# Block means by a dense load and VectorE instead of crossbar turns, in a sparse-attention and GEGLU kernel

## The chip, the cores and the metric

One core of a Trainium2 chip. The metric is the device time of one execution in microseconds (us), as the median of several runs. Lower is better. PE is TensorE's matmul side, PEld its weight loads, DVE is VectorE, ACT is ScalarE, POOL is GpSimd and SP is SyncE, which only issues DMAs here.

## What is computed

Attention over 4 batches, 8 heads, 768 positions and 64 dimensions, then a gated feed-forward layer over the 3072 tokens:

```
k_sum = k.reshape(B, H, nb, 32, D).max(axis=3)
v_sum = v.reshape(B, H, nb, 32, D).mean(axis=3)
scores_l = where(|i - j| < 16, scale * q k^T, -1e9)
scores_s = scale * q k_sum^T + log(32)
a = softmax(concat(scores_l, scores_s))
x = a @ concat(v, v_sum)                     # heads joined: 3072 x 512
out = x + sigmoid(x @ w_res) * ((gelu(x @ w_gate) * (x @ w_val)) @ w_out)
```

The change concerns `v_sum`: the mean of v over each block of 32 positions, 24 blocks for each head.

## The kernel before

Work goes by units of 384 tokens, two to a batch (`NU` = 8, unit u is half u % 2 of batch u // 2). The order of the instructions on every engine is written out by hand in the loop over u (line 532), and each engine works through its own in that order. In iteration u the feed-forward layer of unit u runs, and the attention of unit n = u + 1 is laid between its matmuls.

The iteration starts with twelve fo steps (`fo_step`, L407): for each slice of 128 of the 1536 hidden columns, four matmuls with w_gate (g) and four with w_val (vv) by TensorE, a Gelu by ScalarE (L404), and the product gvT by VectorE (L405). PSUM has four banks ("mm") for g, vv, r, f and part of the scores, taken in turn; so the banks of an fo step are wanted again two steps later. After each fo step `values_step` (L451) and some lines of the loop add work for the next batch. After the twelve steps come, for the next unit, scores (`s_step`: matmuls into s, exponential by ScalarE into P, `mask_part` on VectorE, L347), the product with the values (`av_step`: ao by TensorE, reciprocal and multiplication by VectorE, giving xn), and for the current unit r (L416), f (L432) and the end (`end_step`, L435: two VectorE instructions and the store of 128 rows of out). x must stand transposed (xT) for the next unit's matmuls: either TensorE turns it and ScalarE copies it (`xt_step`, L378), or the DMA crossbar does (`xt_dma`, L385, issued by SP). The first is used for all of x of units 0 to 3, the second for three of four head pairs from unit 4 on (`if u < 3 ... else`, L657); from u = 4 on the first matmuls of a unit (L548) also take the head pair that comes last at the end.

The values and their block means live in `vext[b % 2]`, a tile of 128 rows for each group of 64 queries: 96 rows hold the 96 values in reach, rows 96 to 127 the block means of the batch, the same in each of the 12 groups. `load_values` (L96) loads the values, `v_spread` (L287) copies those which two groups share, and `vsum_bc` (L296) copies the means to the groups, half of the groups at a time. Rows of P over the 24 real blocks are held at zero by a bias of -30000, so what stands in rows 120 to 127 has no weight.

For batches 0 and 1 the means come from TensorE (`vsum_sum`). For batches 2 and 3 they come by this path: `load_rows` (L171) loads v as rows of positions into `v_sb`, eight DMAs of 256-byte pieces issued by POOL; `turn_values` (L258) turns it by four crossbar DMAs into vT in the first fo step of u = 2 or 4; `block_sums` (L265) sums over blocks in fo steps 8 to 11 of the same unit, one head pair at a time; `turn_sums` (L270) turns the sums back by one more crossbar DMA in the first fo step of u = 3 or 5, and `vsum_bc` scales and copies them to the rows of vext: to the first six groups in fo steps 5 to 8 of u = 3 or 5, and to the other six in fo steps 2 to 5 of u = 4 or 6.

k and q are loaded as rows by the same `load_rows` and turned by the crossbar (`turn_batch`, L246: two DMAs for k and one for q for each of the four head pairs). `k_rest` (L206) is five VectorE instructions on a head pair of k: the maxima of the blocks and the copies at the edges of the groups. For batches 2 and 3 three head pairs are turned in u = 2 or 4 and the fourth in u = 3 or 5, and k_rest runs in fo steps 0, 2, 4 and 11 of u = 3 or 5.

POOL issues all loads, in order; a load starts behind a small copy (`gate`, L168) that holds POOL until a given gvT is there. Batch 2 is loaded from u = 1, fo 6 on; batch 3's rows from the end of the fo steps of u = 2 on, and its values at the start of u = 3. POOL also issues the stores of out for u = 3 to 6, SP those of the other units.

Of the kernel before, what the change touches and what calls it, by code (L numbers as in the profile page):

```python
# [9 lines left out]
BF16 = mybir.dt.bfloat16  # L10
# [5 lines left out]
def kernel(  # L16
# [11 lines left out]
    nc = tc.nc  # L28
    B, H, S, D = q.shape
# [45 lines left out]
    vext = [const.tile([128, NT, H, D + 1], BF16, name=f"vext{i}") for i in range(2)]  # L75
    vsum = [const.tile([128, H, D + 1], BF16, name=f"vsum{i}") for i in range(2)]
    tick = const.tile([1, 1], BF16, name="tick")
    vsT = const.tile([128, NP, 128], BF16, name="vsT")
    vsB = const.tile([128, NP, 128], BF16, name="vsB")
    w_gate = wpool.tile([128, KO, DFF], BF16, name="w_gate")  # L80
    w_val = wpool.tile([128, KO, DFF], BF16, name="w_val")
    w_out = wpool.tile([128, FO, DM], BF16, name="w_out")
# [16 lines left out]
        dst = vext[b % 2][0 if c else WIN:128, 2 * c, :, 0:D] if c < NC else vext[b % 2][64:64 + WIN, NT - 1, :, 0:D]  # L99
        nc.gpsimd.dma_start(out=dst, in_=v[b, :, lo:hi, :].rearrange("h p d -> p h d"))  # L100

    k_sb, q_sb, v_sb, vT = {}, {}, {}, {}

    with tc.manual_schedule():

# [63 lines left out]
            nc.gpsimd.tensor_copy(tick[:], t)  # L169

        def load_rows(b):  # L171
            for sb, src, name in ((k_sb, k, "k_sb"), (q_sb, q, "q_sb"), (v_sb, v, "v_sb"))[0:2 if b == 1 else 3]:
                sb[b] = (qk1 if sb is v_sb else qk).tile([128, NP, NC, 2 * D], BF16, tag=name, name=name)
                for h in range(H) if b > 1 else (4, 5, 6, 7, 0, 1, 2, 3):
                    nc.gpsimd.dma_start(out=sb[b][:, h // 2, :, h % 2 * D:h % 2 * D + D],  # L175
                                        in_=src[b, h].rearrange("(c p) d -> p c d", c=NC))

        def load_batch(b):
            load_rows(b)
# [75 lines left out]
                    out=qT[b % 2][hp].rearrange("d (c m) -> d c m", c=NC),  # L255
                    in_=q_sb[b][:, hp].rearrange("p c d -> p (c d)"))

        def turn_values(b):  # L258
            vT = qk1.tile([128, NP, S], BF16, tag="k0", name="vT")
            for hp in range(NP):  # L260
                nc.sync.dma_start_transpose(out=vT[:, hp].rearrange("d (c m) -> d c m", c=NC),
                                            in_=v_sb[b][:, hp].rearrange("p c d -> p (c d)"))
            return vT

        def block_sums(vT, hp):  # L265
            with nc.allow_low_precision("block means are bf16 operands"):
                nc.vector.tensor_reduce(out=vsT[:, hp, 96:96 + NB], in_=vT[:, hp].rearrange("d (n w) -> d n w", w=BLK),
                                        axis=mybir.AxisListType.X, op=ALU.add)

        def turn_sums():  # L270
            nc.sync.dma_start_transpose(out=vsB[:], in_=vsT.rearrange("d p n -> d (p n)"))

        def vsum_sum(b, pool, tag, chunks=range(NC + 1), vs=None, first=True, last=False):
            if vs is None:
# [20 lines left out]

        def vsum_bc(b, hp, lo, hi):  # L296
            dst = vext[b % 2][96:128, lo:hi, 2 * hp:2 * hp + 2, 0:D]
            if b < 2:
                src = vsum[b][96:128, 2 * hp:2 * hp + 2, 0:D]
                nc.vector.tensor_copy(dst, src.unsqueeze(1).to_broadcast([32, hi - lo, 2, D]))  # L300
            else:
                src = vsB[96:128, hp].rearrange("p (h d) -> p h d", d=D)
                nc.vector.tensor_scalar_mul(dst, src.unsqueeze(1).to_broadcast([32, hi - lo, 2, D]), 1.0 / BLK)

        def s_tiles(two=None):
            if two:
# [128 lines left out]
        def end_step(u, st, sub, c0=0, c1=DM):  # L435
            f, th = st["f", sub], st["th", sub][:, c0:c1]
            nc.vector.scalar_tensor_tensor(th, th, 1.0, f[:, 0:c1 - c0], ALU.add, ALU.mult)  # L437
            o = work.tile([128, DM], F32, tag="o", name="o")
            nc.vector.scalar_tensor_tensor(o[:, 0:c1 - c0].rearrange("p (k d) -> p k d", d=128),  # L439
                                           th.rearrange("p (k d) -> p k d", d=128), 0.5,  # L440
                                           st["xn"][:, c0 // 128:c1 // 128, sub, :], ALU.mult, ALU.add)
            row = u * TU + sub * 128
            (nc.gpsimd if 2 < u < NU - 1 else nc.sync).dma_start(out=out[row:row + 128, c0:c1], in_=o[:, 0:c1 - c0])  # L443

        def keep_warm(n, wp=None):
            if wp is None:
# [4 lines left out]
        def values_step(u, fo):  # L451

            b = u // 2 + 1
            if u in (2, 4) and fo >= FO - NP:
                block_sums(vT[b], fo - FO + NP)
            if u in (3, 5):
                if fo in (1, 3):
                    v_spread(b, 0, HT // 2, fo // 2)
                if 5 <= fo < 9:
                    vsum_bc(b, fo - 5, 0, HT)  # L460
            if u % 2 == 0 and u < NU - 1:
                if fo in (0, 1):
                    v_spread(b - 1, HT // 2, NC, fo)
                if 2 <= fo < 2 + NP:
                    vsum_bc(b - 1, fo - 2, HT, NT)


# [64 lines left out]
        for u in range(NU):  # L532
# [2 lines left out]
            n = u + 1  # L535
            if u == 1:
                turn_batch(1, 2, NP)
            if u == 3:
                for c in range(NC + 1):
                    load_values(3, c)  # L540
            gvT = upool.tile([128, FO, TU], BF16, tag="gvT", name="gvT")
            if u > 3:
                firsts = [(w, fo, ps_mm.tile([128, 512], F32, tag="mm", name="gv"))
                          for w, fo in ((w_gate, 0), (w_val, 0), (w_gate, 1))]
                for kos in ((0, 1, 3), (2,)):
                    for w, fo, acc in firsts:
                        for ko in kos:
                            nc.tensor.matmul(acc[:, 0:TU], w[:, ko, fo * 128:(fo + 1) * 128], st["xT"][:, ko, :],  # L548
                                             start=(ko == 0), stop=(ko == 2), skip_group_check=True)
            for fo in range(FO):  # L550
                if u == 0 and fo < 2:
                    for w, _, acc in firsts[2 * fo:2 * fo + 2]:
                        half_fo(st, w, fo, KO - 1, KO, acc)
                    fo_end(gvT, fo, firsts[2 * fo][2], firsts[2 * fo + 1][2])
                elif u > 3 and fo == 0:
                    fo_end(gvT, fo, firsts[0][2], firsts[1][2])
                elif u > 3 and fo == 1:
                    fo_end(gvT, fo, firsts[2][2], half_fo(st, w_val, fo, 0, KO))
                else:
                    fo_step(st, gvT, fo)  # L560
                values_step(u, fo)
                if u == 0 and fo == 4:
                    nc.vector.memset(vsT[:], 0.0)
                    load_rows(1)
                if u == 0 and fo == 6:
                    vext_consts(1)
                if u == 0 and fo == FO - 1:
                    kw_consts(1)
                    for c in range(NC + 1):
                        load_values(1, c)  # L570
                if u == 2 and fo == FO - 1:
                    gate(gvT[0:1, fo, 0:1])
                    load_rows(3)
                if half == 0 and 1 < nb < B and fo == 0:
                    vT[nb] = turn_values(nb)
                    turn_batch(nb, 0, NP - 1)
                if half == 1 and 1 < nb < B and fo == 0:
                    turn_sums()
                    turn_batch(nb, NP - 1, NP)
                if half == 1 and 1 < nb < B and fo in (0, 2, 4, 11):  # L580
                    k_rest(kW[nb % 2][(0, 2, 4, 11).index(fo)])
                if u == 1 and fo == 6:
                    gate(gvT[0:1, fo, 0:1])
                    load_batch(2)
                if u == 1 and fo in (1, 2, 6, 7):
                    home = TT if fo % 2 else AO
                    if fo < 4:
                        k_step(nb, fo - 1, *home)
                    else:
                        q_step(q_sb[nb], nb, 0, S, fo - 6, *home)  # L590
                if u == 1 and fo == FO - 1:
                    k_rest(kW[1][2])
                    k_rest(kW[1][3])
                if u == 0 and fo >= FO - 4:
                    k_later(kW[0][fo - FO + 4])
                if u == 0 and fo in (FO - 3, FO - 2):
                    for hp in range(2 * (fo - FO + 3), 2 * (fo - FO + 3) + 2):
                        q_step(qb, 0, TU, S, hp, *(TT if hp % 2 else AO))
# [55 lines left out]
            av_step(n, 1, nst, *TT)  # L654
            s_step(n, 2, nst)
            s_step(n, 3, nst, two=(MM, MM), masked=False)
            if u < 3:  # L657
                if u > 1:
                    end_step(u, st, 0)
                mask_part(3, nst)  # L660
                m = 6 if u > 1 else 9
                ffn_step(st, gvT, 1, 0 if u > 1 else 6, m)
                xt_step(n, 0, nst, *AO, nc.scalar.copy)
                ffn_step(st, gvT, 1, m, FO)
                xt_step(n, 1, nst, *TT, nc.scalar.copy)
                res_step(st, 2)
                av_step(n, 2, nst, *AO)
# [5 lines left out]
            else:  # L673
# [2 lines left out]
                mask_part(3, nst)  # L676
                end_step(u, st, 0)
                ffn_step(st, gvT, 1, 0, FO)
                av_step(n, 2, nst, *AO)
                xt_dma(2, nst)  # L680
                av_step(n, 3, nst, *TT)
# [37 lines left out]
```

The softmax here doesn't subtract the row's maximum and nothing guards it: scores larger than these inputs give would overflow.

## Time and profile before

| | |
|---|---|
| median of 3 runs | 260.31 us (258.98, 260.31, 260.67) |
| the profiled execution | 259.77 us, of which the span from the first to the last instruction is 257.9 us |
| granted TensorE clock | 1.0 of full speed |
| busy, share of the span | PE 97%, DVE 69%, PEld 54%, ACT 50%, POOL 39% |
| DMA bytes | 30.16 MB in 117899 packets, of which 104816 under 512 bytes |
| chain that ended last, by engine | PE 79%, DVE 7%, DMA 5%, POOL 4%, issue 2%, ACT 1% |

The span begins with the first instruction and ends with the last. Units begin, by the first matmul of their fo steps, at about 24.1 (u = 0), 51.7, 84.2, 113.1, 142.4, 170.7, 199.4 and 227.7 us (u = 7). In the lines of a timeline the first two numbers are the start and the duration in us, then the engine, the source line, the operation, what is written and what is read, and the count; in brackets the idle time before it and what ended it. A group's line names the operation and ends with busy us, mean ns of one instruction, and the idle time before it. Durations of instructions that follow each other can overlap, since VectorE and TensorE are pipelined: the pace is the distance from start to start. In the chain of waits overlaps are taken out.

### The profile page before, as it was taken

What the parts mean: (1) busy time and instruction counts of PE and PEld (TensorE: products, weight loads), DVE (VectorE), ACT (ScalarE), POOL (GpSimd) and SP (SyncE); (2) the same over time, 40 slices, a digit from 0 to 9 for tenths busy, and PEclk for the clock granted to TensorE, in tenths of its full rate; (3) what the DMA queues carried; (4) which work ended last, traced back from release to release, by engine and by line L of the source; (5) the groups of instructions that cost most, each with busy time, mean ns of one, the idle gap of its engine ahead of it and who ended that gap; (6) DMA issues with size and microseconds to landing.
All of it is one profiled execution on the core that took longest, in us unless ns stands there. A gap on an engine that the chain in (4) does not pass through costs nothing.

```text
span 257.9 us, 5755 instructions
## 1 busy us (share of the span) xinstructions
PE 250.2 (97%) x2249; PEld 139.5 (54%) x2249; DVE 178.3 (69%) x426; ACT 129.5 (50%) x223; POOL 101.0 (39%) x139
## 2 busy tenths in 40 slices
PE   7989999999999999999999999999999999999993
PEld 3546555566545555555554565555554665556543
DVE  5756866595598878679959768679768853764333
ACT  4855369455635637553373537453473537443310
POOL 7995542795699910996650100020001000010000
PEclk9999999999999999999999999999999999999999
DMA  7999999999999999999994995165003200130012
GB/s 157 151 151 193 199 202 199 142 209 123 151 152 165 179 129 167 125 186 202 154 134 90 146 145 103 31 153 68 1 3 86 84 0 0 33 137 3 1 41 83
DMA packets 117899, 30.16 MB, mean 117 GB/s; under 512 B 104816, under 2 KB 115504, under 8 KB 117872
## 3 DMA queue, kind: packets, MB, share of 16 engines
q0 software_dynamic: 86640, 19.11, 86.7%
q1 hardware_dynamic: 31232, 10.69, 25.6%
q8 instruction: 17, 0.28, 0.5%
q14 instruction: 10, 0.08, 0.1%
HBM read 32.51 MB, written 6.29 MB: 150 GB/s over the span
## 4 chain that ended last, share of the span: by engine, by line
PE 79%; DVE 7%; DMA 5%; POOL 4%; issue 2%; ACT 1%; POOLq 0%; DVEq 0%
PE f L432 22%; PE vv L398 19%; PE g L398 18%; PE r L416 8%; PE ao L362 3%; DMA k_sb<-in_k_dram 3%; PE gv L548 3%; DMA vext<-in_v_dram 2%; PE s L330 2%; DVE gvT L405 2%; PE xp L381 1%; POOL k_sb L175 1%; POOL vext L100 1%; DVE ks L211 1%; DVE vext L294 1%
## 5 line engine op out<-in xcount | busy, mean ns | idle before, releaser
L398 PE MATMUL vv<-xT,w_val 128*128 128x384 bf16 x364 | 74.5, 326 | 0.1
L404 ACT ACTIVATE ge<-g 128x384 f32<-128x384 f32 x87 | 42.7, 491 | 63.3 <-PE g L398 37.0
L398 PE MATMUL g<-xT,w_gate 128*128 128x384 bf16 x348 | 71.3, 326 | 0.4 <-DVE gvT L405 0.2
L405 DVE TENSOR_TENSOR gvT<-ge,vv 128x384 bf16<-128x384 f32 x91 | 50.0, 553 | 27.5 <-PE vv L398 25.5
L432 PE MATMUL f<-w_out,gvT 128*128 128x512 bf16 (+2 forms) x312 | 68.4, 363 | 0.0
L398 PEld LDWEIGHTS <-w_val 128*128 128x128 bf16 x368 | 36.0, 98 | 24.0 <-issue 0.4
L398 PEld LDWEIGHTS <-w_gate 128*128 128x128 bf16 x352 | 34.1, 98 | 23.2 <-issue 1.1
L432 PEld LDWEIGHTS <-gvT 128*128 128x128 bf16 x312 | 28.3, 98 | 28.2
L443 POOL DMA_DIRECT2D out_dram<-o x12 | 6.5, 544 | 90.9 <-DVE rz L370 76.0
L422 ACT ACTIVATE th<-r 128x512 f32<-128x512 f32 x24 | 14.2, 602 | 24.8 <-PE r L416 24.8
L437 DVE SCALAR_TENSOR_TENSOR th<-th,f 128x512 f32<-128x512 f32 (+2 forms) x26 | 16.7, 642 | 12.3 <-PE f L432 8.5
L175 POOL DMA_DIRECT2D k_sb<-in_k_dram x24 | 19.8, 839 | 12.5 <-DMA w_out<-in_moe_w_out_dram 5.2
L416 PE MATMUL r<-w_res,xT 128*128 128x512 bf16 x96 | 24.4, 380 | 0.0
L100 POOL DMA_DIRECT2D vext<-in_v_dram x28 | 23.2, 875 | 1.5 <-PE g L398 1.2
L175 POOL DMA_DIRECT2D q_sb<-in_q_dram x24 | 20.0, 875 | 1.6 <-DMA k_sb<-in_k_dram 1.4
L347 DVE TENSOR_TENSOR P<-P,maskt 128x768 bf16<-128x768 bf16 x28 | 15.3, 556 | 7.2 <-ACT P L336 3.9
L372 DVE TENSOR_TENSOR xn<-ao,rz 128x384 bf16<-128x384 f32 x32 | 17.8, 558 | 1.1
L383 ACT COPY xT<-xp 128x384 bf16<-128x384 bf16 x20 | 9.3, 482 | 16.5 <-PE xp L381 14.8
L439 DVE SCALAR_TENSOR_TENSOR o<-th,xn 128x512 f32<-128x512 f32 (+2 forms) x26 | 16.9, 651 | 0.9
L336 ACT ACTIVATE P<-s,bias_t 128x384 bf16<-128x384 f32 x32 | 16.8, 579 | 1.3 <-PE s L330 1.3
L339 ACT ACTIVATE P<-s,bias_t 128x768 bf16<-128x768 f32 x16 | 14.5, 904 | 3.5 <-PE s L330 3.4
L175 POOL DMA_DIRECT2D v_sb<-in_v_dram x16 | 13.2, 850 | 2.8 <-DMA q_sb<-in_q_dram 2.5
(99 smaller groups left out, 236.0 us busy)
## 6 DMA issues: line engine op xcount, KB each, us to landing
out_dram<-o POOLq DMA_DIRECT2D x12, 256.0 KB, 2.4
out_dram<-o SPq DMA_DIRECT2D x11, 256.0 KB, 4.2
vext<-in_v_dram POOLq DMA_DIRECT2D x20, 128.0 KB, 7.4
k_sb<-in_k_dram POOLq DMA_DIRECT2D x24, 96.0 KB, 7.7
q_sb<-in_q_dram POOLq DMA_DIRECT2D x24, 96.0 KB, 5.5
w_gate<-in_moe_w_gate_dram POOLq DMA_DIRECT2D x6, 256.0 KB, 8.5
w_val<-in_moe_w_val_dram POOLq DMA_DIRECT2D x6, 256.0 KB, 9.1
w_out<-in_moe_w_out_dram POOLq DMA_DIRECT2D x3, 512.0 KB, 14.9
```

Source lines behind the costliest of these rows:

```text
L100: nc.gpsimd.dma_start(out=dst, in_=v[b, :, lo:hi, :].rearrange("h p d -> p h d"))
L175: nc.gpsimd.dma_start(out=sb[b][:, h // 2, :, h % 2 * D:h % 2 * D + D], in_=src[b, h].rearrange("(c p) d -> p c d", c=NC))
L336: nc.scalar.activation(P[:, hh].rearrange("p t q -> p (t q)"), s[hh][:, 0:TU], AF.Exp, scale=scale, bias=bias_t[:])
L347: nc.vector.tensor_mul(Pf, Pf, maskt.unsqueeze(1).to_broadcast([128, 2 * HT, QT]))
L372: nc.vector.tensor_mul(xn, ao[:, :, :, 0:D], rz.to_broadcast([128, NSUB, 2, D]))
L398: nc.tensor.matmul(acc[:, 0:TU], w[:, ko, fs], st["xT"][:, ko, :], start=(ko == 0), stop=(ko == KO - 1))
L404: nc.scalar.activation(ge[:], g[:, 0:TU], AF.Gelu)
L405: nc.vector.tensor_mul(gvT[:, fo, :], ge[:], vv[:, 0:TU])
L416: nc.tensor.matmul(r[:], st["xT"][:, ko, ss], w_res[:, ko, :], start=(ko == 0), stop=(ko == KO - 1))
L432: nc.tensor.matmul(st["f", sub][:, 0:c1 - c0], gvT[:, fo, ss], w_out[:, fo, c0:c1], start=(fo == 0), stop=(fo == FO - 1))
L437: nc.vector.scalar_tensor_tensor(th, th, 1.0, f[:, 0:c1 - c0], ALU.add, ALU.mult)
L439: nc.vector.scalar_tensor_tensor(o[:, 0:c1 - c0].rearrange("p (k d) -> p k d", d=128), th.rearrange("p (k d) -> p k d", d=128), 0.5, st["x ...
```

## The change

- The row load of v, its crossbar turns, and the turn of the sums are gone. `v_sb` for batches 2 and 3 has one partition for each pair of head and block (4 heads x 24 blocks = 96) and for each of two groups of heads, with the 32 x 64 values of the block one after the other: two DMAs from POOL, whose rows are dense in memory.
- `block_means` sums over the 32 positions on VectorE, a quarter of the work in each of fo steps 8 to 11 of u = 2 and 4, and a second instruction scales the means and writes them six times, for six groups of queries.
- `spread_means` puts them on their rows of vext by eight plain DMAs from SP, one for each head: for the first six groups in fo step 2 of u = 3 and 5, for the other six in fo step 0 of u = 4 and 6. `vsum_bc` is left for batches 0 and 1 only.
- `v_spread` in u = 3 and 5 moves from fo steps 1 and 3 to 2 and 7.
- All four head pairs of k and q are turned in the first fo step of u = 2 and 4. `k_rest` of pair 0 moves to the end of u = 2 and 4, in front of the last two av_step; that of the others is in fo steps 0, 4 and 11 of u = 3 and 5.
- Batch 3 is loaded, all together, from u = 3, fo 0 on.
- x of unit 3 goes by `xt_dma` for three of four head pairs, in the order that later units have; the first matmuls of u = 3 are ordered as those of later units are.
- The stores of out of u = 2 go by POOL.

```diff
-    vsT = const.tile([128, NP, 128], BF16, name="vsT")
-    vsB = const.tile([128, NP, 128], BF16, name="vsB")
+    vds = const.tile([PP, 2, D], BF16, name="vds")
+    vdt = const.tile([128, 2, HT, D], BF16, name="vdt")
...
-            for sb, src, name in ((k_sb, k, "k_sb"), (q_sb, q, "q_sb"), (v_sb, v, "v_sb"))[0:2 if b == 1 else 3]:
-                sb[b] = (qk1 if sb is v_sb else qk).tile([128, NP, NC, 2 * D], BF16, tag=name, name=name)
+            for sb, src, name in ((k_sb, k, "k_sb"), (q_sb, q, "q_sb")):
+                sb[b] = qk.tile([128, NP, NC, 2 * D], BF16, tag=name, name=name)
...
+            if b > 1:
+                v_sb[b] = qk1.tile([PP, 2, BLK, D], BF16, tag="k0", name="v_sb")
+                for g in range(2):
+                    nc.gpsimd.dma_start(out=v_sb[b][:, g].rearrange("p w d -> p (w d)"),
+                                        in_=v[b, 4 * g:4 * g + 4].rearrange("h (n w) d -> (h n) (w d)", w=BLK))
...
-        def block_sums(vT, hp):
+        def block_means(b, i):
+
+            g, d = i // 2, slice(i % 2 * 32, i % 2 * 32 + 32)
             with nc.allow_low_precision("block means are bf16 operands"):
-                nc.vector.tensor_reduce(out=vsT[:, hp, 96:96 + NB], in_=vT[:, hp].rearrange("d (n w) -> d n w", w=BLK),
+                nc.vector.tensor_reduce(out=vds[0:PP, g, d], in_=v_sb[b][:, g, :, d].rearrange("p w d -> p d w"),
                                         axis=mybir.AxisListType.X, op=ALU.add)
-        def turn_sums():
-            nc.sync.dma_start_transpose(out=vsB[:], in_=vsT.rearrange("d p n -> d (p n)"))
+            nc.vector.tensor_scalar_mul(vdt[0:PP, g, :, d], vds[:, g, d].unsqueeze(1).to_broadcast([PP, HT, 32]), 1.0 / BLK)
+
+        def spread_means(b, lo, hi):
+
+            for h in range(H):
+                nc.sync.dma_start(out=vext[b % 2][96:128, lo:hi, h, 0:D],
+                                  in_=vdt[h % 4 * NB:h % 4 * NB + 32, h // 4])
...
-            (nc.gpsimd if 2 < u < NU - 1 else nc.sync).dma_start(out=out[row:row + 128, c0:c1], in_=o[:, 0:c1 - c0])
+            (nc.gpsimd if 1 < u < NU - 1 else nc.sync).dma_start(out=out[row:row + 128, c0:c1], in_=o[:, 0:c1 - c0])
...
             if u in (2, 4) and fo >= FO - NP:
-                block_sums(vT[b], fo - FO + NP)
-            if u in (3, 5):
-                if fo in (1, 3):
-                    v_spread(b, 0, HT // 2, fo // 2)
-                if 5 <= fo < 9:
-                    vsum_bc(b, fo - 5, 0, HT)
+                block_means(b, fo - FO + NP)
+            if u in (3, 5) and fo in (2, 7):
+                v_spread(b, 0, HT // 2, fo // 7)
+                if fo == 2:
+                    spread_means(b, 0, HT)
             if u % 2 == 0 and u < NU - 1:
                 if fo in (0, 1):
                     v_spread(b - 1, HT // 2, NC, fo)
-                if 2 <= fo < 2 + NP:
+                    if fo == 0 and u > 2:
+                        spread_means(b - 1, HT, NT)
+                if 2 <= fo < 2 + NP and u < 4:
                     vsum_bc(b - 1, fo - 2, HT, NT)
...
-            if u == 3:
-                for c in range(NC + 1):
-                    load_values(3, c)
...
-            if u > 3:
+            if u > 2:
                 firsts = [(w, fo, ps_mm.tile([128, 512], F32, tag="mm", name="gv"))
...
-                if u == 2 and fo == FO - 1:
+                if u == 3 and fo == 0:
                     gate(gvT[0:1, fo, 0:1])
-                    load_rows(3)
+                    load_batch(3)
                 if half == 0 and 1 < nb < B and fo == 0:
-                    vT[nb] = turn_values(nb)
-                    turn_batch(nb, 0, NP - 1)
-                if half == 1 and 1 < nb < B and fo == 0:
-                    turn_sums()
-                    turn_batch(nb, NP - 1, NP)
-                if half == 1 and 1 < nb < B and fo in (0, 2, 4, 11):
-                    k_rest(kW[nb % 2][(0, 2, 4, 11).index(fo)])
+                    turn_batch(nb, 0, NP)
+                if half == 1 and 1 < nb < B and fo in (0, 4, 11):
+                    k_rest(kW[nb % 2][(0, 4, 11).index(fo) + 1])
...
-            if u < 3:
-                if u > 1:
-                    end_step(u, st, 0)
+            if u == 1:
...
                 end_step(u, st, 0)
                 ffn_step(st, gvT, 1, 0, FO)
+                if u in (2, 4):
+                    k_rest(kW[nb % 2][0])
                 av_step(n, 2, nst, *AO)
```

The last lines are those of the `else` branch, which u = 2 now takes.

## The prediction

> **What bounds the kernel now.** I read the page's busy shares first, then the windows table with one window per unit of 384 tokens (units 2 to 5), then VectorE's timeline in the last four fo steps of unit 4, then TensorE's timeline just behind it.
>
> ```profile
> PE 250.2 (97%) x2249; PEld 139.5 (54%) x2249; DVE 178.3 (69%) x426; ACT 129.5 (50%) x223; POOL 101.0 (39%) x139
> ```
>
> TensorE is busy 97% of 257.9 us, so only stalls inside that figure, and PE work, can be won.
>
> ```profile
> 84.20:113.06 28.86, 28.86 (x254) 16.21 (x253) 22.07 (x40) 15.62 (x28) 17.68 (x23) 1.00 1.90 153
> 113.06:142.40 29.34, 28.87 (x245) 15.73 (x244) 23.75 (x56) 14.33 (x25) 16.00 (x21) 1.00 1.85 149
> 142.40:170.75 28.35, 28.35 (x245) 15.74 (x244) 21.25 (x40) 14.19 (x25) 1.61 (x4) 1.00 0.68 109
> 170.75:199.35 28.60, 28.53 (x245) 15.74 (x244) 22.80 (x56) 14.21 (x25) 1.62 (x4) 1.00 0.29 57
> ```
>
> The columns: length, then busy time of PE, PEld, DVE, ACT, POOL. Units 3, 4 and 5 have the same 245 PE records and take 29.34, 28.35 and 28.60: 28.35 is the floor, units 3 and 5 lose 0.99 and 0.25. The chain of waits says where: in unit 3, from 120.23 to 126.21 us it runs over DVE (gvT, vext L294, km, ks, vext L303), else over PE. Unit 2 has 9 more records and 0.5 more time: x of unit 3 turned by PE.
>
> ```profile
> 154.19 0.56 DVE L405 TENSOR_TENSOR gvT<-ge,vv 128x384 bf16<-128x384 f32 x1 [0.74 <-PE vv L398]
> 154.66 0.95 DVE L267 TENSOR_REDUCE vsT<-vT 128x24 bf16<-128x768 bf16 x1
> 155.53 0.54 DVE L405 TENSOR_TENSOR gvT<-ge,vv 128x384 bf16<-128x384 f32 x1
> ...
> 158.63 0.95 DVE L267 TENSOR_REDUCE vsT<-vT 128x24 bf16<-128x768 bf16 x1
> 160.11 0.56 DVE L347 TENSOR_TENSOR P<-P,maskt 128x768 bf16<-128x768 bf16 x1 [0.53 <-ACT P L339]
> 161.05 0.56 DVE L347 TENSOR_TENSOR P<-P,maskt 128x768 bf16<-128x768 bf16 x1 [0.39 <-ACT P L336]
> ```
>
> ```profile
> 157.92 0.52 PE L330 MATMUL s<-qT,kW 64*128 64x64 bf16 x24
> 158.37 1.04 PE L416 MATMUL r<-w_res,xT 128*128 128x512 bf16 x4
> 159.25 2.75 PE L432 MATMUL f<-w_out,gvT 128*128 128x512 bf16 x12
> 161.84 1.03 PE L416 MATMUL r<-w_res,xT 128*128 128x512 bf16 x4
> 162.79 0.57 PE L362 MATMUL ao<-vext,P 128*64 128x65 bf16 x24
> ```
>
> Here the block sums run already. An fo step of PE is 1.30 us (8 matmuls, 0.65 per 4 in the chain). DVE needs 0.47 for gvT, from start to next start, and 0.86 for a reduce: 1.33, so it holds pace. The two masks must be done before ao at 162.79; the second ends at 161.61. That is the only cover there is.
>
> [...] The trace agrees: 768 elements take 948 ns (L267), 384 take 553 (L211), so 1.03 ns an element and some 0.15 us fixed. [...]
>
> **Gains.** (a) Unit 3: four vsum_bc (0.36 to 0.66) leave fo 5 to 8, one of four k_rest (1.3 to 2.0) leaves, v_spread moves to fo 2 and 7; the worst step left is fo 0 with one k_rest. So unit 3 falls to the floor: -0.99. The same in unit 5: -0.25. (b) x of unit 3 by crossbar: nine transposes leave PE, -0.5 (28.86 to 28.35); three ACT copies of 0.48 leave too, and ACT is idle half the time. Sum -1.7. (c) Eight v_sb row DMAs per batch become two dense ones, four vT transposes and one vsB transpose leave SP: DMA time falls, but it lies beside PE, which waits for no DMA in the table of waits. In unit 4 and 6 the vsum_bc removed were hidden (unit 4 is at the floor): nothing.
>
> **Costs, at the floor already.** (d) block_means in fo 8 to 11 of units 2 and 4. Each is a reduce of 96x1024 down to 32, read over w with a step of 64 bf16, 128 bytes, so every element is a hop, and a scaled copy of 192 elements. The copy: 288 elements took 218 ns (L215), 768 took 380 (L303), on that line 0.19. [...] With 0.04 between the two and 0.09 overlap with the next, x = reduce + 0.14 of the queue: 1.36, 2.06 or 2.85. From gvT of fo 8, DVE then needs 4 x (0.47 + x) for the steps and 0.47 + 0.56 for two masks: 2.91 + 4x. PE reaches the second pair of ao 8.67 + 0.25 = 8.92 us after it (162.86 in the chain less 154.19). Stall per unit: 4x - 6.0. At 1.36 none (0.5 to spare), at 2.06 2.25, at 2.85 5.4. gvT of fo 10 and 11 are late for f too (PSUM bank and operand), which is the same lag met earlier, not added. Break-even for any stall is a reduce of 1.36 us, for the whole change 1.55. [...] Two units: +4.5.
>
> (e) k_rest of pair 0 moves to the tail of units 2 and 4 (1.22 us, from 130.20 to 131.42), in front of av_norm of pairs 2 and 3. xn of pair 3 then ends at 170.07 where xp starts at 169.99: 0.1 a unit. xt_dma of pair 2 lands 2.3 us after issue, at 171.7, needed for the last gv matmuls at 172.21. The end steps behind it slide 1.2 too, and their banks are wanted 0.4 to 0.5 later. +0.2; were it slowed by POOL to 2.0, +1.4, but POOL has no load then.
>
> (f) SP. In unit 4 behind the third xT turn (to 141.1): eight spreads, issue 0.33 to 0.56 each as SP's plain out DMAs, 4.5 at most, then twelve turns of 1.3, 15.6: free at 161.2, and xt_dma of unit 5 is ready at 164.15. In unit 2 twelve turns from 85.5 on; nine with their gaps took 13.6 and the four in front of them, waiting for loads, 8.8, so some 20: free at 105.9, xt_dma ready at 105.9, x needed at 112.9. Cover 3 us and more; without it PE waits for each us. In units 3, 5 and 6 the spreads have 15 us to their ao. Nothing.
>
> (g) POOL. Batch 3 starts at 115.2 instead of 102.7. Before, 31 DMAs were issued in 30 us. 16 for k and q at 1.16 us each (the pace while the ring was full, 116.1 to 125.4) are in by some 136; two v are issued by 138 and land, with the slowest v_sb row of before (10.6), by 149; seven vext are issued by 145 at worst. Wanted: turns at 145, block means at 154, v_spread at 175. Were v late, the first reduce would hold every gvT queued behind it on DVE, and PE within 1.3 us. Unit 2's three outs go to POOL, which is idle there; unit 3's wait behind the loads, up to one unit, with three o buffers. Nothing.
>
> **Sum.** -1.7 + 4.5 + 0.2 = +3.0. On the profiled execution's own 259.77 (span 257.9 and 1.9 around it) that is 262.8; it stands 0.5 under the median of 260.31, so 263.3.
>
> **Rivals.**
> A, not slower: the hop is free and the reduce costs 1.22. [...] Then -1.7 + 0.2: 258.8. It decides below a reduce of 1.55 us.
> B, the forecast: 263.3.
> [...]
> D: a queue decides. Should a spread cost over 1.4 us of SP's issue (192 short runs, where out has 128 long ones), xt_dma of unit 5 comes too late, and every 0.1 above costs 0.8; at 2 us some 5, on B 268. Against: SP's 0.33 hardly knows the size.
> The change also may not ease unit 3: then A is 259.8, B 264.3.
>
> **How the numbers follow.** A 0.22, B 0.46, C 0.26, D 0.06. B alone spans 262 to 265.5, by the slack read to 0.3 us a unit and hops of 1.65 to 2.0 ns. The range reaches down over nearly all of A and up to where C begins to bite in full: 258.2 to 269.0, leaving out half of C and A's edge. About 1% is what a measurement of this kernel can tell from no change, 2.6 us: slower is D, C and two thirds of B, 0.63; within it most of A and a third of B, 0.34; faster is A with luck, 0.03, as the sum of all gains is 1.7.
>
> **What would show it.** The TENSOR_REDUCE of 96x1024: 1.9 us (B), 1.2 (A), 2.7 (C). Windows of units 2 and 4 at 30.6, unit 3 and 5 at 28.4; ao in units 2 and 4 waiting for the mask, in the chain DVE's reduces in fo 8 to 11. SP's spreads at 0.3 to 0.6. I am wrong if the reduce is over 1.55 and units 2 and 4 still keep 28.4, or if unit 3 stays at 29.3.

## The result, and the profile after

The changed kernel takes 271.58 us (median of 4, 269.06 to 274.42) beside 260.40 us for the kernel before: 1.041 times, 95% interval 1.032 to 1.049. The longest of the four counts as slow and is left out of this ratio; the median of the other three is 271.29. It is slower, and above the forecast's range, which ended at 269.0. The profiled execution took 271.87 us with a span of 270.2, 12.3 more than before.

The windows of units 2 to 5 (the columns as before, and behind them the granted clock, the DMA share and GB/s; a unit begins where its first matmuls would begin, so a wait of theirs counts to it):

```profile
85.73:118.05 32.32, 30.50 (x244) 16.33 (x243) 27.01 (x49) 14.30 (x25) 2.56 (x5) 0.95 0.99 116
118.05:146.42 28.37, 28.37 (x244) 15.73 (x243) 20.66 (x47) 14.18 (x25) 22.00 (x30) 1.00 1.69 134
146.42:183.66 37.24, 32.47 (x245) 16.48 (x244) 24.90 (x45) 14.29 (x25) 1.50 (x3) 0.91 0.55 94
183.66:212.02 28.36, 28.36 (x244) 15.72 (x243) 20.74 (x48) 14.18 (x25) 1.75 (x4) 1.00 0.18 49
```

Unit 3 and unit 5 came down to the floor as forecast (29.3 and 28.6 before). Unit 2 lost 3.4 and unit 4 lost 8.9 us. Units 0 and 1 are 1.7 longer and the last is 0.5 shorter. The 1.7 is for the most part spread between executions: unit 2 begins at 84.0, 84.5 and 84.9 us in the three traces that have the code of before up to there, and at 84.1 to 85.8 in the eleven that have the changed code. The sum: 1.7 + 3.4 - 1.0 + 8.9 - 0.2 - 0.5 = 12.3.

The groups show the instruction in dispute:

```profile
L267 DVE TENSOR_REDUCE vds<-v_sb 96x32 bf16<-96x1024 bf16 x8 | 15.2, 1905 | 0.0
L269 DVE TENSOR_SCALAR vdt<-vds 96x192 bf16<-96x192 bf16 x8 | 1.6, 206 | 0.3
```

1.905 us was forecast as 1.92, the scaled copy of 0.206 as 0.19. The timeline of TensorE in unit 2 shows what it does:

```profile
105.92 0.39 PE L432 MATMUL f<-w_out,gvT 128*128 128x512 bf16 x1 [0.48 <-DVE gvT L405]
106.14 1.03 PE L416 MATMUL r<-w_res,xT 128*128 128x512 bf16 x4
108.43 0.97 PE L362 MATMUL ao<-vext,P 128*64 128x65 bf16 x24 [1.26 <-DVE P L347]
```

TensorE waits for the last gvT and then for the mask, as forecast. The same timeline at the start of unit 4 shows what was not in the forecast:

```profile
145.99 0.59 PE L432 MATMUL f<-w_out,gvT 128*128 128x512 bf16 x2
148.21 0.32 PE L546 MATMUL gv<-xT,w_gate 128*128 128x384 bf16 x1 [1.63 <-DMA xT<-xn]
149.08 0.48 PE L546 MATMUL gv<-xT,w_gate 128*128 128x384 bf16 x2 [0.55 <-DMA xT<-xn]
149.41 0.65 PE L546 MATMUL gv<-xT,w_val 128*128 128x384 bf16 x3
149.89 1.10 PE L546 MATMUL gv<-xT,w_gate 128*128 128x384 bf16 x3
151.77 0.48 PE L546 MATMUL gv<-xT,w_gate 128*128 128x384 bf16 x1 [0.78 <-DMA xT<-xn]
...
152.68 1.48 PE L398 MATMUL vv<-xT,w_val 128*128 128x384 bf16 x4
153.96 1.48 PE L398 MATMUL g<-xT,w_gate 128*128 128x384 bf16 x4
155.24 1.48 PE L398 MATMUL vv<-xT,w_val 128*128 128x384 bf16 x4
156.52 0.95 PE L398 MATMUL g<-xT,w_gate 128*128 128x384 bf16 x4
```

Three times the matmul stands and waits for a turn of x; behind that a group of four matmuls takes 1.28 us from start to start in place of 0.65: half the clock, until some 157 us. The three turns landed 7.7 to 8.2 us after issue; before, all twelve took 2.3 to 2.4. POOL issued the loads of batch 3 from 121.77 (k_sb) to 141.9 (the last of its values); the turns were issued between 139.98 and 145.2.

### The profile page after: what moved, and what is told of

Its sections match the earlier page's. It is cut to its first block, busy times and chain, and to the rows that moved or that the text cites. A ratio compares the mean times of both kernels' runs of the same rounds, so it can differ in the third digit from the quotient of the medians.

```text
span 270.2 us, 5773 instructions
## 1 busy us (share of the span) xinstructions
PE 255.4 (95%) x2240; PEld 140.2 (52%) x2240; DVE 180.8 (67%) x418; ACT 128.0 (47%) x220; POOL 92.0 (34%) x130
## 4 chain that ended last, share of the span: by engine, by line
PE 74%; DVE 9%; DMA 8%; POOL 4%; issue 1%; ACT 1%; POOLq 0%; DVEq 0%
PE vv L398 20%; PE g L398 19%; PE f L432 18%; PE r L416 6%; DVE vds L267 4%; PE gv L546 3%; DMA k_sb<-in_k_dram 3%; PE ao L362 3%; DMA xT<-xn 3%; DMA vext<-in_v_dram 2%; PE s L330 2%; POOL k_sb L175 1%; PE xp L381 1%; POOL vext L100 1%; DVE gvT L405 1%
## 5 line engine op out<-in xcount | busy, mean ns | idle before, releaser
L405 DVE TENSOR_TENSOR gvT<-ge,vv 128x384 bf16<-128x384 f32 x90 | 49.4, 553 | 37.3 <-PE vv L398 36.3
L404 ACT ACTIVATE ge<-g 128x384 f32<-128x384 f32 x85 | 41.7, 490 | 64.0 <-DVE gvT L405 35.6
L398 PE MATMUL g<-xT,w_gate 128*128 128x384 bf16 x340 | 70.5, 329 | 0.0
L432 PE MATMUL f<-w_out,gvT 128*128 128x512 bf16 (+2 forms) x312 | 69.5, 367 | 0.9 <-DVE gvT L405 0.9
L443 POOL DMA_DIRECT2D out_dram<-o x15 | 8.2, 547 | 124.3 <-DVE km L214 56.7
L267 DVE TENSOR_REDUCE vds<-v_sb 96x32 bf16<-96x1024 bf16 x8 | 15.2, 1905 | 0.0
L383 ACT COPY xT<-xp 128x384 bf16<-128x384 bf16 x17 | 7.9, 481 | 15.4 <-PE xp L381 13.7
```

The source lines that it names most:

```text
L267: nc.vector.tensor_reduce(out=vds[0:PP, g, d], in_=v_sb[b][:, g, :, d].rearrange("p w d -> p d w"), axis=mybir.AxisListType.X, op=ALU.add)
L398: nc.tensor.matmul(acc[:, 0:TU], w[:, ko, fs], st["xT"][:, ko, :], start=(ko == 0), stop=(ko == KO - 1))
L404: nc.scalar.activation(ge[:], g[:, 0:TU], AF.Gelu)
L405: nc.vector.tensor_mul(gvT[:, fo, :], ge[:], vv[:, 0:TU])
L432: nc.tensor.matmul(st["f", sub][:, 0:c1 - c0], gvT[:, fo, ss], w_out[:, fo, c0:c1], start=(fo == 0), stop=(fo == FO - 1))
```

## The experiments

Two losses stand side by side, so the first four runs take one away each, or make one alone. Each run was compared with the kernel before on the same chip (260.35 us for these four). My theory: VectorE's lag costs some 2.3 us in each of units 2 and 4, and the loads of batch 3, moved a unit later, run into the turns of x of unit 4. The rival: the lag is the whole loss, and the wait is another face of it.

**No hops.** The reduce reads neighbours.

```diff
-in_=v_sb[b][:, g, :, d].rearrange("p w d -> p d w")
+in_=v_sb[b][:, g, i % 2 * 16:i % 2 * 16 + 16].rearrange("p w (a c) -> p (w a) c", c=BLK)
```

> The changed kernel with one edit: each reduce reads 1024 elements that lie one after the other in place of 1024 that lie 128 bytes apart, and gives 32 sums of neighbours; so the block means of batches 2 and 3 are not the reference's, everything else is. Theory: two separate losses, VectorE's lag in units 2 and 4 (2.3 us each, with TensorE at half its clock for some 1.8 us after it in unit 2) and a wait for x of unit 4 at the start of unit 4. The reduce falls from 1.91 to 1.22 us, the lag goes, the wait for x stays: 271.6 - 4.6 - 1.8 = 265.2. Rival, VectorE's lag is the whole loss: 259. Rival, hops are not what makes the reduce slow: 1.9 us still and 271.6.

264.58 us, 1.015 (1.008 to 1.023). The line of the reduce, from the instructions on this tile (minimum, median and maximum):

```profile
L267 DVE TENSOR_REDUCE vds<-v_sb x8: 1205/1208/1209, 97.0 to 166.5; 96x32 bf16<-96x1024 bf16 x8
```

Same bytes, same count, 0.70 us less: the hop of 128 bytes costs 0.68 ns an element. No wait for a mask or gvT is left in the table of TensorE's waits; its wait for x of unit 4 is (4.5 us). So the lag is real: 6.7 us go with it, counted from 271.29, and unit 2 keeps its clock. What this run and the next two take away adds up to more than the whole loss of 10.9, in part since the half clock of unit 2 is gone in all three.

**Values later.** The rows of batch 3 stay in unit 3.

```diff
+                if u == 4 and fo == 2:
+                    gate(gvT[0:1, fo, 0:1])
+                    for c in range(NC + 1):
+                        load_values(3, c)
```

> The changed kernel with the seven loads of the values of batch 3 moved from the start of unit 3 to the third fo step of unit 4; the rows of k, q and v stay in unit 3. Theory: the crossbar turns of x of unit 4 land 8 us after issue because their packets share the DMA engines with these loads; now most of the loads are through, the turns land in 2.3 to 4 us, TensorE waits for less than 1.5 us in place of 4.5 and keeps its clock: some 266. Rival, the turns are late for a reason of SP or of the crossbar itself: they land in 8 us again and the time stays at 271.6.

263.80 us, 1.013 (1.009 to 1.018): better than expected. The turns of x of unit 4 land in 2.4 to 4.2 us, TensorE waits for none of them, and the granted clock is 1.0 throughout. The turns themselves and SP's order did not change, so it is the traffic of the loads that delayed them. What is left in this run is the lag alone: units 2 and 4 of its trace last 30.9 us each:

```profile
85.31:116.21 30.90, 28.94 (x241) 15.63 (x243) 26.35 (x49) 14.29 (x25) 1.24 (x3) 1.00 1.05 111
144.57:175.47 30.90, 28.94 (x242) 15.62 (x244) 24.88 (x45) 14.19 (x25) 7.51 (x11) 1.00 1.03 117
```

**x of unit 4 by TensorE**, as the kernel before has it for units 1 to 3 (`xt_step` for `xt_dma` at u = 3, and the first matmuls in plain order).

> The changed kernel with x of unit 4 turned by TensorE, in the order that the kernel before has in that place. Theory: the wait for x (4.5 us) and the slow clock behind it (2.0) go, nine transposes come back (0.5): 265.6, with the reduce and the lag in units 2 and 4 as they are. Rival, the loss at the start of unit 4 comes from something other than x (an operand from the loads, the clock by itself): TensorE still stands there and the time stays within 2 us of 271.6.

263.53 us, 1.013 (1.008 to 1.018). Here the loads are where the change put them, and only the operand that was late goes another way. Both runs land on the same time, 7.5 and 7.8 below the changed kernel's 271.29, and some 2 better than expected. Not all of it is the collision. In the traces, units 3 and 4 together take 65.6 us in the changed kernel and 59.3 with the values late: 6.3 less (5.8 here, where TensorE has the nine transposes back). Unit 2 gives 1.4 more, since its clock fell in the trace of the changed kernel and in neither of these.

**One part in the kernel before: late loads.**

```diff
-                if u == 2 and fo == FO - 1:
+                if u == 3 and fo == 0:
                     gate(gvT[0:1, fo, 0:1])
-                    load_rows(3)
+                    load_batch(3)
```

> The kernel before with one part of the change alone: all loads of batch 3, its v rows among them, start after the first fo step of unit 3. Theory: 31 loads of 256-byte pieces now run until some 152 us, over the turns of x of unit 4 at 136 to 142 and those of v at its start; the turns land late, TensorE waits 4 to 7 us and then runs at half its clock for 2 to 4: 266 to 270. Rival, VectorE's lag alone carries the loss of the change: 260.4, as before.

263.10 us, 1.011 (1.006 to 1.016): slower alone, with no block mean on VectorE, but by at most half of what I expected. The turns of x land in 4.9 to 5.9 us, TensorE waits 1.8 for them and keeps its clock. In this kernel the values come behind eight v row loads: the first turn was issued at 136.2, ahead of the first load of values at 137.3, where in the changed kernel five loads of values and the two of v were in flight. That this makes the turns less late is not shown; this part of my size was a guess.

**Matmuls into the gap**, to see what the half clock follows. Twenty matmuls of zeros stand in front of the first of unit 4 in the changed kernel (`keep_warm(20, ...)` into the bank of ao).

> The changed kernel with twenty matmuls of zeros (0.216 us each, 4.3 in all) laid in front of the first matmuls of unit 4, into a bank that nobody reads. They delay nothing as long as x of unit 4 is not there, which takes 5 us. Theory: the clock of TensorE falls to half because it stands idle for so long, and the slow matmuls behind the wait (4 at 1.28 us in place of 0.65) cost some 2 us; filled with matmuls the clock holds: 271.6 - 2 to 2.5, some 269.3. Rival, the fall of the clock has nothing to do with the idle time: the slow stretch stays and the time with it, 271.6, or is 1 longer.

269.21 us, 1.035 (1.029 to 1.041), against 1.041 without them; the intervals overlap. TensorE's timeline there:

```profile
143.32 4.48 PE L449 MATMUL wp<-warm 128*128 128x512 bf16 x20
147.63 0.65 PE L548 MATMUL gv<-xT,w_gate 128*128 128x384 bf16 x3
...
149.54 0.32 PE L548 MATMUL gv<-xT,w_gate 128*128 128x384 bf16 x1 [0.28 <-DMA xT<-xn]
...
150.03 0.81 PE L398 MATMUL vv<-xT,w_val 128*128 128x384 bf16 x4
150.68 0.81 PE L398 MATMUL g<-xT,w_gate 128*128 128x384 bf16 x4
```

x is as late as in the changed kernel (a turn lands 8.9 us after issue), but the groups of four keep their 0.65. So the fall of the clock follows the idle time. Units 3 and 4 of the traces take 65.6 us without the added matmuls and 64.0 with them; the medians can't give the size, since in unit 2 as well the clock fell in the first trace and not in the second (32.3 and 30.9).

How much idle time it takes can be read from the granted clock, the number behind the busy times. In the trace of the changed kernel it falls at 109.00 and at 149.96, for 3.41 and 6.83 us:

```profile
105.59:109.00 3.41, 1.73 (x23) 0.77 (x25) 3.37 (x6) 0.60 (x1) 0.00 (x0) 1.00 0.45 79
109.00:112.41 3.41, 3.41 (x42) 1.80 (x43) 2.49 (x7) 1.84 (x3) 0.00 (x0) 0.50 0.16 36
146.54:149.96 3.42, 1.24 (x8) 0.65 (x7) 1.38 (x2) 1.41 (x2) 0.84 (x2) 1.00 1.85 201
149.96:153.37 3.41, 2.63 (x10) 1.08 (x9) 0.56 (x1) 0.94 (x2) 0.00 (x0) 0.50 0.50 151
```

The two falls are 41.0 us apart, twelve times 3.41, a third stretch begins behind the last matmul at 269.4, 35 times 3.41 after the second, and in every trace with more than one stretch at half clock they begin whole multiples of 3.41 apart. If each trace is divided into such steps, and idle time is a step's length less the busy time of PE, a fall between the start of unit 0 and the last unit came only behind a step in which TensorE was idle for 1.7 us or more: 1.7 and 2.2 here, 2.6 in the run without hops, 3.2 and 1.9 in two runs further down (x of unit 3 by the crossbar, and the second with halving additions). Behind steps with up to 1.66 us the clock held. The longest of these is in unit 4 of the run with late values:

```profile
163.80:167.21 3.41, 1.75 (x8) 0.41 (x6) 3.34 (x7) 0.65 (x2) 0.00 (x0) 1.00 0.66 109
```

So the lag's two stalls, 1.7 us together, lie at the edge, and what one step holds of them depends on where the steps lie: with the same stalls in unit 2 the clock fell in this trace and held in three others. No exact limit comes out; in the last unit steps with up to 1.9 us idle had no fall behind them.

**Another part in the kernel before: x of unit 3 by the crossbar**, with the loads left where they were (`u < 2` for `u < 3`, `u > 2` for `u > 3`).

> The kernel before with one part of the change alone: x of unit 3 by the crossbar for three of four head pairs, in the order of later units; the loads stay where they are, so the rows of batch 3 load from 102.7 us on, over these turns. Theory: turns that run beside a stream of row loads land in 5 to 9 us in place of 2.3; TensorE waits at the start of unit 3 and may lose its clock after it: 263 to 267. Rival, the lateness in the changed kernel came from the mixture of 128-byte spreads and v loads that only it has: x of unit 3 is there in time, nine transposes leave TensorE, 259.8.

266.07 us, 1.021 (1.015 to 1.027). The turns land in 6.8 to 7.2 us, TensorE waits 4.2 for them and its clock falls. So neither the spreads nor the dense loads are needed for the collision: turns of x beside a stream of row loads have it here too. It also shows why the two edits go together: the rows of batch 3 left the tail of unit 2 for x of unit 3, and met x of unit 4 instead.

**Both losses taken away.** `block_means` becomes halving additions, which read rows of 64 neighbours:

```diff
+                for m in (16, 8) if i % 2 == 0 else (4, 2, 1):
+                    nc.vector.tensor_add(t[:, g, 0:m], t[:, g, 0:m], t[:, g, m:2 * m])
+            if i % 2:
+                nc.vector.tensor_scalar_mul(vdt[0:PP, g], t[:, g, 0:1].to_broadcast([PP, HT, D]), 1.0 / BLK)
```

Once with x of unit 3 by TensorE, k and q of batch 3 at the end of unit 2, v and the values at the start of unit 3 (and the stores of out of unit 2 by SP, as before), and once with the values late, as above.

> The changed kernel with the sums taken as five halving additions of neighbouring rows (16, 8, 4, 2, 1 rows of 64, in place) in two fo steps each, in place of reduces over hops; x of unit 3 by TensorE and the rows of k and q of batch 3 at the end of unit 2, as before, v and the values at the start of unit 3. Theory: additions of 1024, 512, 256, 128 and 64 elements at two a cycle come to 1.1 and 1.0 us an fo step, under the 1.5 that the masks allow, and no turn of x runs over a load: units 3 and 5 at 28.4, nothing lost elsewhere: 259.2, 1.2 under the kernel before. Rival, the spreads or the denser loads cost something of their own that the lag hid: 261 or more.

259.70 us, 0.998 (0.996 to 1.000).

> The changed kernel with the same halving additions and with the values of batch 3 loaded from the third fo step of unit 4 on; x of unit 3 by the crossbar as changed. Theory: with both losses gone what is left are the gains that the forecast counted, 1.7: units 2 to 5 at 28.4 each, 258.5. Rival, only one of the losses can be taken away at a time (the values now run over the turns of x of unit 5): 261 to 264.

261.40 us, 1.007 (1.004 to 1.009). The additions of 1024 and 512 elements take 0.68 and 0.42 us, 0.51 ns an element between them where the reduces of the kernel before took 1.03 (how many go to a cycle no trace shows), and no wait for a mask is left. Yet both are slower than I expected, and both where unit 5 begins, with waits for x of 0.45 us in the first and 1.9 in the second. SP's timeline in the first of them:

```profile
146.78 5.30 SPq L277 DMA_DIRECT2D vext<-vdt  x8
152.20 2.51 SPq L258 DMA_TRANSPOSE kW<-k_sb  x2
...
167.51 1.23 SPq L261 DMA_TRANSPOSE qT<-q_sb  x1
168.91 3.80 SPq L389 DMA_TRANSPOSE xT<-xn  x3
```

The spreads begin behind a copy that VectorE makes in the first fo step (`v_spread`), some five microseconds later than I had put them, at 0.66 us from one to the next; the twelve turns of k and q follow, and x of unit 5, ready at 164.8, is issued at 168.9. In the changed kernel VectorE's lag had hidden this, since there x of unit 5 was ready only at 176.8.

**The spreads out of that queue**, in fo step 7 of units 3 and 5.

```diff
-                if fo == 2:
-                    spread_means(b, 0, HT)
+                spread_means(b, fo // 7 * HT, HT + fo // 7 * HT)
...
-                    if fo == 0 and u > 2:
-                        spread_means(b - 1, HT, NT)
```

> The run with halving additions and late values, with one more edit: the second eight spreads go out in fo step 7 of units 3 and 5, where SP has nothing else to do, in place of the first fo step of units 4 and 6. In the run without this edit SP started the eight spreads of unit 4 at 145.3 us, behind a copy of VectorE in the first fo step, not at 141, and the twelve turns behind them ended at 168.7; x of unit 5, ready at 163.8, was issued 5 us late and TensorE waited 1.9 us and lost part of its clock. Theory: that queue on SP was the rest of the loss: unit 4 falls from 30.7 to 28.4 and the time from 261.4 to some 259. Rival, the values that load from 147 on make the turns of x late: still 261.

259.17 us, 0.996 (0.994 to 0.998).

> The run with halving additions, x of unit 3 by TensorE and k and q early, with the same edit: the second eight spreads in fo step 7 of units 3 and 5. Without it unit 4 lasted 29.3 us in place of 28.4, since x of unit 5 was issued 4 us late on SP. Theory: unit 4 falls to the floor, 259.7 - 0.9 = 258.8, 1.2 to 1.5 under the kernel before. Rival, x of unit 5 is late because k_rest stands in front of the last av_norm: no gain, 259.7.

258.47 us, 0.994 (0.992 to 0.996). Both as expected, and no wait for x is left in either. These two leave out an order: the spreads go ahead of the copy that takes the values out of the same rows for the second six groups, so batches 2 and 3 get wrong values there.

**The copy ahead of the spreads.** It moves to fo step 6 of units 3 and 5.

> The run with halving additions, k and q early, and the second spreads in unit 3 and 5; in that run the spreads came ahead of the copy that moves the values out of those rows for the second six groups, so out of batches 2 and 3 was not the reference's. Here that copy (0.70 us of VectorE) moves from the first fo step of units 4 and 6 to fo step 6 of units 3 and 5, ahead of the spreads. Theory: fo steps 6 and 7 of units 3 and 5 hold 0.47 + 0.70 us of VectorE each, under 1.30, so nothing changes: 258.5. Rival, VectorE falls behind there as it did in unit 3 of the kernel before: 259 to 260.

258.76 us, 0.995 (0.993 to 0.997).

> The same edit on the run with late values and x of unit 3 by the crossbar, which is the changed kernel with its three losses taken away: the additions for the hops, the values after the turns of x of unit 4, the spreads out of SP's queue in unit 4. Theory: units 2 to 5 at 28.4, 259.2 as without the edit or a little less, against 271.6 for the change as it was made; the gains that the forecast counted, 1.7, are there once nothing takes them back. Rival, the copy in unit 5 waits for the late values and holds VectorE: over 260.

259.11 us, 0.997 (0.995 to 0.999). The windows of units 2 to 5 of this last run, which has all parts of the change with its three losses taken out:

```profile
84.11:112.61 28.50, 28.50 (x245) 15.67 (x244) 22.05 (x53) 14.29 (x25) 2.40 (x4) 1.00 1.10 129
112.61:140.97 28.36, 28.36 (x244) 15.74 (x243) 22.44 (x49) 14.19 (x25) 16.31 (x23) 1.00 1.40 139
140.97:169.47 28.50, 28.50 (x244) 15.64 (x243) 19.84 (x48) 14.18 (x25) 7.51 (x11) 1.00 0.99 120
169.47:197.84 28.37, 28.37 (x245) 15.75 (x243) 21.43 (x49) 14.18 (x25) 1.78 (x4) 1.00 0.23 56
```

Units 3 and 5 are at the floor, units 2 and 4 within 0.15 of it. The four together are 1.4 us shorter than before; the forecast's gains less its 0.2 for k_rest were 1.5. The whole span, 256.2, is 1.7 under that of before, but this execution is the second shortest of 22 (257.89 to 261.73 us), so that nearness to the forecast is in part luck. The medians give 1.1 us for this version and 1.5 for the one with x of unit 3 by TensorE, and their intervals overlap.

## Why the prediction was wrong

- **Gains (a), (b): right.** Units 3 and 5 fell to the floor, by 1.0 and 0.2 us, and what the nine transposes gave shows in unit 2 of the last run, 28.50 in place of 28.86.
- **(d), the lag: right in mechanism and size.** The reduce took 1.905 us for 1.92. Units 2 and 4 of the run with late values last 30.9 us, those of the last run without the lag 28.5: 2.4 each for a forecast of 2.25. No reduce in the trace of before runs over hops, so no trace stands behind the 1.92 of the sum (2.06 in the queue), nor behind the 2.85 and the 1.65 to 2.0 ns of the range. The runs showed 1.905 us over hops and 1.208 over neighbours, 0.68 ns an element more; 1.905 less the 0.15 fixed of the reduces before is 1.71 ns an element, an estimate. That it would be this size and not 2.7 us, the forecast could not know; it gave it 0.46. The two runs without the collision, 263.8 and 263.5, stand where the forecast stood, 263.3.
- **(g), the loads a unit later: the step that failed.** I wrote that the last values would be issued by 145 at worst, asked only whether the readers of the loaded data would wait, and put "Nothing". Who else uses the DMA engines in that time was not asked, and the turns of x at the end of unit 3 stand in no term of the sum. In (e) I counted a turn of x as 2.3 us, the figure of a trace in which none had met the stream in full: the twelve were issued from 135.8 us on, when POOL had issued its last load at 132.1 and only the tail of it was in flight, until 137.7. The turns of k and q, many of which did run beside loads, stood in the table of DMA issues with 5.1 and 5.5 us to landing, and the profile's DMA slices were nine tenths full until 135 us. (c) leaned on the same trace: PE waited for no DMA in it. The runs show what the loads do to them: the turns land in 7.7 to 8.2 us beside the loads and in 2.4 to 4.2 when the values come later. In place of nothing it cost 4.3 us until the first twelve matmuls of unit 4 were done (the group behind them starts at 152.68, where 148.4 was due) and 2.1 more at half clock behind them: 6.4, where the traces of the changed kernel and of the run with late values differ by 6.3 in units 3 and 4. The 1.16 us an issue I put down to a full ring, which the trace does not show: there POOL waited 0.45 to 0.85 us for landings of q_sb ahead of four of these issues, and in the changed kernel the sixteen for k and q took 13.2 us, 0.83 each.
- **The clock: not in the forecast at all.** Each us of stall was counted as one. In unit 4, and in the profiled execution in unit 2 also (f took 3.82 us in place of 2.59, and with it 1.4 us were lost there), idle time was followed by matmuls at half speed. The traces show the granted clock in steps of 3.41 us, and a step need not be idle throughout: 1.7 and 2.2 us of it were enough.
- **(f), SP: "Nothing" was wrong, and hidden.** A spread costs 0.60 us of SP's issue and 0.66 from one to the next, not 0.33 to 0.56, and the eight of unit 4 wait for a copy of VectorE. With the lag gone this cost 1.4 and 2.4 us, each run taken against the kernel before on its own chip. Of rival D the place was right, the price not: the queue comes too late through that wait, with a spread far under 1.4 us.
- **(e): right.** In the last run xp of units 2 and 4, whose tails have k_rest, starts 0.1 us later behind the f in front of it than in unit 3, and these units are 0.13 us longer than units 3 and 5; 0.1 a unit was forecast.
- **VectorE slowed by POOL**, the 1.4 that (e) named beside its 0.2, was not shown: in the kernel before, the L213 copy took 0.57 and 0.59 us at 116.36 and 119.67 and 0.20 at 123.00, and all three started while POOL was issuing loads (from 116.11 to 116.93, 117.78 to 120.24 and 122.34 to 123.16). No term of the sum rests on it.
- Rivals A and C are out by the reduce itself: 1.905 us, where A had 1.2 and C 2.7. What stays open is whether a few tenths of the 1.7 us in units 0 and 1 have a cause; the code there is the same but for one clearing of a tile that is 0.1 us longer and, late in unit 1, fewer loads.
- **The sum.** The forecast had +3.0, the two traces +12.3. Of the 9.3 between, 6.3 are the collision with its half clock, 1.4 the half clock in unit 2, 1.2 the first two units (1.7) and the last (-0.5), and 0.4 a lag a little longer than forecast, in both units together.

## What to carry to other kernels

When a stream of loads is moved, ask of every other DMA in its new time whose landing is on the path, and not only of those that read the loaded data; a landing time holds only for the traffic beside which it was measured (for a turn of x 2.3 us on quiet DMA engines, 7.7 to 8.2 beside the loads). When a stall is priced on TensorE, add the half clock that may follow it (1.4 and 2.1 us in the changed kernel's trace). And a cost that lies behind a larger one shows only when the larger is gone, so follow each queue to its last instruction even where the first estimate says that it is covered.

## What the runs showed of the hardware

- A VectorE reduce of bf16 that hops 128 bytes at each element took 1.908 us (median) for 1024 elements, and 1.208 over neighbours: 1.58 times.
- Two-input additions of bf16 rows took 0.68, 0.42, 0.28 and 0.22 us for 1024, 512, 256 and 128 elements (256, 128 and 64 in a row 0.76), so 0.51 ns an element from 512 to 1024. The sums by halving need about 1.9 us where two reduces over hops take 3.8.
- A crossbar turn of x took 2.3 us to land on quiet DMA engines. Beside POOL's loads it took 4.9 to 5.9 us (kernel before, late loads), 6.8 to 7.2 (kernel before, x of unit 3) and 7.7 to 9.8 (changed kernel, without hops, and with matmuls in the gap).
- After stalls of nearly the same shape (0.5 and 1.3 us, within 3.0 us) the clock fell once, in unit 2 of the changed kernel's trace, and held seven times, in unit 2 of three other runs and in unit 4 of four. The traces show the clock in steps of 3.41 us; ahead of the last unit it fell behind steps with 1.68 us or more of idle time, and held behind those with 1.66 or less.
